# Sooner gated product in each half's last unit, moved steps in three queues, and fp16 copies of exponentials on ScalarE in the long units of the second half

## The chip, the cores and the metric

The kernel runs on one core of one Trainium2 chip. The metric is the device time of one execution in microseconds (us): 1716.42 us for the kernel before, the median of three runs (1714.65 to 1716.99).

Engines are named as in the profile: PE is TensorE (matmuls), PEld its weight loads, DVE is VectorE, ACT is ScalarE, POOL is GpSimd, SP is SyncE, which starts the transfers. L12 is line 12 of the kernel before, unless a sentence says that a line number is of the changed kernel.

## The reference

An input x of 2048 rows and 576 columns goes through two branches, and a gate per row mixes them:

```python
g = _sigmoid((x * gate_w).sum(-1, keepdims=True))
a = _A_ref(x, A_wq, A_wk, A_wv, A_wo, A_beta)
b = _B_ref(x, B_w_gate, B_w_up, B_w_down)
return g * a + (1 - g) * b
```

Branch A is attention with 32 heads of width 18, in four segments of 512 rows. In a segment each head does causal softmax attention, and mixes it with a read of a memory that holds phi(k)^T v of the segments before; a matmul with wo ends the branch. Branch B is `(silu(x @ w_gate) * (x @ w_up)) @ w_down` with an inner width of 4608.

## The kernel before, in words

One program does four stages on one core, and PE is meant to run through all of them.

**Segments (0 to 233.5 us).** For each of the four segments come nine chains `qk` (14 matmuls of 512 columns into one of three shared banks of PSUM, L223), whose results ACT and DVE turn into queries, keys and phi of both (L455 to L468), and then eight `v_step` with `mem_step`. Beside the chains of segments 1 to 3, `upd_gen` adds the last segment to the memory: PE transposes phi (L513, L516), the pieces are copied to `kt` by ACT (512 columns, L514) and DVE (the last 64 columns, L517), and PE multiplies `kt` with the values (L505). Also beside the chains, pieces of x are summed on POOL and split into fp16 pairs on ACT and DVE for the next stage: `first_sum`, `first_split`, `rest_sum` (POOL, L654), `rest_split` (ACT L248, DVE L249). Tables such as `RSTEP`, `FSUM` and `FSPLIT` say beside which chain each stands.

**First half (233.5 to 921.5 us).** The inner width is cut in 36 units f of 128, and the rows in two halves of 1024. A unit makes the gate and up products of a half by seven products of a Strassen-like scheme: `seven(t, j)` is product j, seven matmuls of 512 columns (L1426, L1429). Copies of finished products go to ACT (L1519, L1526, L1533, L1537, with SiLU L1540 and L1542), sums to DVE (L1530, L1538). After product 6, DVE forms the two parts of the gated product, `sg0` from bank and silu (L1548) and `sg1` from `p5` and silu (L1549; product 6 is not read there). `split_by` splits each part into fp16 high (`hh`, ACT L1295) and low (`hl`, DVE L1298) in later ticks.

Between two products stands a `tick` with eight beats k. A tick runs what `defer` put off to it, and starts steps of the plan: weights of the next unit (`w_make`: POOL L369, ACT L373, DVE L377), and the down weights: `d_look` measures them (ACT L1116), `d_scale` makes their scale (a PE step L158, then POOL), `d_split` makes three fp16 tiles `dw` (ACT L1139, DVE L1140, then L1142 on DVE or L1144 on ACT).

Every third unit (f = 3, 6, ..., 33) is long, 34 to 39 us where the others take 10.6 to 14.7. In it stand the 16 down groups of the three chunks before: a group is nine matmuls (L1162) into one of two banks, which DVE then adds into `ya` (L1171, or L1169 for the first). Unit 35 feeds a further 16, which run in it and in ten beats behind it. Attention runs inside the ticks as a generator, `att_gen`, one step at a time: scores (PE L889), maximum (DVE L907), scores again transposed (PE L1002), the exponential (ACT L1006), its fp16 copy `p1` (DVE L1102, or ACT L1104), the remainder `p2` (POOL L1106), and the products with the values (PE L1030, L1032). Score banks are three.

**Second half (921.5 to 1640 us).** The same 36 units with the other 1024 rows. Here some attention steps are "turned": the scores are kept (DVE L897), ACT takes the exponential (L943), DVE makes an fp16 copy (`c_bank`, L947), POOL the remainder (L948), a transfer transposes both, and PE multiplies (L964, L965; sums L975 on DVE). After that the output tail with wo ends the kernel at 1717 us.

`exp_table` is a small ACT activation (L1419) that brings the table of the exponential in early; SiLU needs another table, so each change of function costs an ACT_TABLE_LOAD. `gates` (L1413 and its DVE steps L1414 to L1416) forms the mixing gate, once, in unit 3 of the first half. `rest_second` prepares the last rows of x for the second half in unit 35 and the beats behind it (ACT L1388, DVE L1392, POOL sums L1381).

Of the kernel before, what the change touches and what calls it, by code (L numbers as in the profile page):

```python
# [17 lines left out]
AF = mybir.ActivationFunctionType  # L18
# [51 lines left out]
def gated_mix(ctx, tc, xT, xrest, wf, wfr, wfh, wd, wv, wo, beta, cmask, ident, bmask, out):  # L70
# [323 lines left out]
    with ExitStack() as st:  # L394
# [101 lines left out]
        def upd_gen(s):  # L496
            acc = [pair_tile([P, 3, MW]), pair_tile([P, 2, MW])]
            Mo, Mn = Mm[s % 2], Mm[(s + 1) % 2]
            for i in range(5):
# [8 lines left out]
                if i < 4:  # L508
# [8 lines left out]
                    nc.vector.tensor_copy(kt[:, 512:576], tb[:, 64:128])  # L517
# [143 lines left out]
        RSTEP = {2: (0, 3), 3: (5, -1), 4: (1, -4), 5: (4, -2), 6: (2,), 7: (-6,), 8: (6,)}  # L661
# [59 lines left out]
        def scan_load(t):  # L721
# [3 lines left out]
            if t in (21, 30):  # L725
# [3 lines left out]
        FSUM = {3: [(1, 0), (4, 0)], 4: [(2, 0), (1, 1)], 6: [(4, 1), (2, 1)], 7: [(6, 0)], 8: [(6, 1)]}  # L729
        FSPLIT = {2: [(0, 0)], 3: [(5, 0), (0, 1)], 4: [(1, 0), (4, 0)], 5: [(5, 1), (2, 0)], 6: [(1, 1), (3, 0)],  # L730
                  7: [(3, 1), (4, 1)], 8: [(2, 1)]}
        for s in range(NSEG):
            upd = upd_gen(s - 1) if s else None
            casts = []
            for n, (m, u) in enumerate(chains):
# [41 lines left out]
                qk(s, m, u, mid)  # L777
                flush(2)
# [19 lines left out]
            for n in range(8):  # L798
# [23 lines left out]
                else:  # L822
                    if n == 4:
                        wraw_of[1] = [w_load(1, u) for u in range(2)]
                    if n < 2:
                        first_split(6, n)
# [8 lines left out]
                    for _ in range((0, 0, 2, 1, 2, 2, 2, 2)[n]):  # L835
                        if start[0][0] < 8:
                            start.pop(0)[1]()
# [5 lines left out]
    with ExitStack() as st:  # L843
# [101 lines left out]
        def c_bank(u, n):  # L945
            lg, pq = homes["lg"][n], spot("pq", u, n)
            nc.vector.tensor_copy(pq[:, 0:L], lg)  # L947
# [103 lines left out]
        def att_gen():  # L1051
            N = 10 * NB
            for tau in range(N + TL + VL + 5):
# [44 lines left out]
                if 0 <= z < N and z // 5 not in turned:  # L1098
                    pe = cur.pop(z)
                    p1 = ap.tile([P, L], F16, name="p1", bufs=6)  # L1100
                    if later[0] or z % 5 not in turn_of[0]:
# [188 lines left out]
        later = [False]  # L1290
        turn_of = [()]
# [33 lines left out]
        def feed(half, f):  # L1325
            return [(f // CH, i, hf, hs, ds, half) for i in range(8) for hf in range(2)]
# [43 lines left out]
        def rest_second(rest):  # L1370
# [19 lines left out]
            def low(j):  # L1390
# [3 lines left out]
            todo = [(-1, load, 0), (0, high, 0), (0, high, 3), (1, low, 0), (1, low, 3), (4, load, 1), (11, high, 5),  # L1394
                    (11, total, 1), (12, low, 5), (12, high, 1), (13, total, 4), (13, low, 1), (14, total, 2),
                    (14, high, 4), (15, low, 4), (15, total, 6), (16, high, 2), (16, low, 2), (17, high, 6), (18, low, 6)]
# [37 lines left out]
        for pos, (half, f) in enumerate(seq):  # L1434
# [49 lines left out]
            def tick():  # L1484
# [5 lines left out]
                if half == 0:  # L1490
# [3 lines left out]
                    if (f == 2 and k < CH) or (f > 2 and q == 0 and 2 <= k < 2 + CH):  # L1494
                        d_look(k if f == 2 else f + k - 2)
                    if (f, k) == (2, 3) or (f > 2 and (q, k) == (0, 5)):
                        d_scale(f // CH)
                    if (f, k) == (2, 7) or (f > 2 and (q, k) == (1, 3)):
                        d_back(f // CH)
                    if f == 2 and k > 4 or f > 2 and (q, k) in ((1, 1), (1, 7), (2, 5 + int(f < FT - 1))):  # L1500
                        g = k - 5 if f == 2 else f - 1 if k == 1 else f
# [8 lines left out]
            later[0] = half == 1 and f > 0  # L1510
            turn_of[0] = () if pos < 24 else (1, 3)
# [154 lines left out]
```

## Time and profile before

| what | value |
|---|---|
| median of three runs | 1716.42 us (1714.65 to 1716.99) |
| the profiled execution | 1718.78 us |
| its span, first to last instruction | 1717.1 us |
| PE busy | 1679.5 us, 98% of the span |
| DVE busy | 1353.8 us, 79% |
| ACT busy | 1076.6 us, 63% |
| POOL busy | 889.2 us, 52% |
| mean granted PE clock | 0.998 |

The span leaves 1.68 us of the profiled execution outside. Busy shares are means over stages with different limits, so the prediction reads them stage by stage. A timeline row gives the start in us from the span's start, the duration in us, engine, line, operation and tiles, and in brackets how long the engine was idle before and what ended the wait. A row of a wait table gives who waited for whom, the sum in us, how often, and the longest.

### The profile page before, as it was taken

Reading aid. Unit: us, or ns where it says so; the run is one execution under the profiler, and the core shown is the slowest. Engines: PE = TensorE matmul, PEld = TensorE weight load, DVE = VectorE, ACT = ScalarE, POOL = GpSimd, SP = SyncE. Lnnn points to the kernel's source line nnn. Section 1 sums busy time; section 2 is a strip of 40 time slices with the busy share of each in tenths; the row PEclk is TensorE's granted clock in tenths of the full one; section 3 lists DMA queues with packets and bytes.
Section 4 is the critical chain, followed back from the end, with each engine's and each line's share of the span. In section 5 each row is a group of like instructions: output and inputs, shape, how many; then the busy total and the mean of one; then the engine's idle time right before and its main releaser. Section 6 shows DMA issues by size and latency. Waiting matters only on the chain.

```text
span 1717.1 us, 35318 instructions
## 1 busy us (share of the span) xinstructions
PE 1679.5 (98%) x12269; PEld 1077.8 (63%) x12269; DVE 1353.8 (79%) x3295; ACT 1076.6 (63%) x1930; POOL 889.2 (52%) x1191
## 2 busy tenths in 40 slices
PE   9999999999999999999999999999999999999999
PEld 7898865556655665565555656556656656655577
DVE  6687676789888988898886878788878788776466
ACT  7666567777777777767774654665556566565411
POOL 3336562266667665665452665465546565554121
PEclk9999999999999999999999999999999999999999
DMA  8666675666776675446535486796696597574544
GB/s 282 218 232 222 214 260 208 208 200 177 231 223 208 168 244 192 154 121 195 169 123 164 114 192 158 163 219 136 147 215 166 121 221 167 140 163 125 156 157 145
DMA packets 349542, 314.25 MB, mean 183 GB/s; under 512 B 201268, under 2 KB 266548, under 8 KB 349364
## 3 DMA queue, kind: packets, MB, share of 16 engines
q1 hardware_dynamic: 349364, 312.00, 63.5%
q8 instruction: 96, 1.57, 0.4%
q14 instruction: 82, 0.67, 0.1%
HBM read 186.15 MB, written 99.55 MB: 166 GB/s over the span
## 4 chain that ended last, share of the span: by engine, by line
PE 73%; DVE 12%; ACT 7%; issue 3%; DMA 3%; POOL 1%; SPq 1%; DVEq 0%; ACTq 0%; POOLq 0%
PE bank L1426 31%; PE bank L1162 18%; PE bank L223 8%; PE bank L1429 5%; PE bank L889 3%; PE bank L1002 2%; DVE ya L1171 1%; PE bank L1030 1%; ACT L1540 1%; DVE junk L907 1%; PE bank L1032 1%; PE bank L964 1%; DVE p L1102 1%; ACT row L1540 1%; DMA rc<-rt 1%
## 5 line engine op out<-in xcount | busy, mean ns | idle before, releaser
L1162 PE MATMUL bank<-dw,hh 128*128 128x320 f16 (+1 forms) x2304 | 437.5, 286 | 13.3 <-DVE ya L1171 8.9
L1162 PE MATMUL bank<-dw,hl 128*128 128x320 f16 (+1 forms) x1152 | 330.1, 287 | 3.8 <-DVE hl L1298 3.2
L1106 POOL TENSOR_TENSOR p<-pe,p 128x512 f16<-128x512 f32 x220 | 271.9, 1236 | 75.3 <-DVE p L1102 50.6
L1162 PEld LDWEIGHTS <-hh 128*128 128x128 f16 x2304 | 225.3, 98 | 99.9 <-issue 18.1
L1006 ACT ACTIVATE pe<-bank 128x512 f32<-128x512 f32 x220 | 130.1, 592 | 183.6 <-PE bank L1002 167.5
L1171 DVE SCALAR_TENSOR_TENSOR ya<-bank,sc,ya 128x320 f32<-128x320 f32 x352 | 176.2, 511 | 55.0 <-PE bank L1162 53.3
L1429 PE MATMUL bank<-xr,rh 128*128 128x512 f16 x504 | 191.0, 379 | 0.0
L907 DVE CUSTOM_DVE_ANT_0 junk<-bank,cm 128x128 bf16<-128x128 f32 (+2 forms) x352 | 169.3, 481 | 13.7 <-PE bank L889 7.3
L1298 DVE SCALAR_TENSOR_TENSOR hl<-hh,row 128x512 f16<-128x512 f16 x144 | 129.7, 902 | 45.7 <-ACT hh L1295 44.8
L1014 POOL TENSOR_SCALAR_AFFINE_SELECT pe<-pe 128x256 f32<-128x256 f32 (+1 forms) x220 | 89.3, 406 | 144.9 <-ACT pe L1006 137.3
L1162 PEld LDWEIGHTS <-hl 128*128 128x128 f16 x1152 | 112.7, 98 | 34.3 <-DVE hl L1298 3.8
L889 PE MATMUL bank<-kst,qst 108*128 108x512 bf16 (+3 forms) x512 | 124.5, 299 | 3.6 <-ACT pe L1006 2.9
L1002 PE MATMUL bank<-qst,kst 111*128 111x512 bf16 (+3 forms) x352 | 103.2, 300 | 1.1 <-DVE acc L975 1.1
L1102 DVE CAST p<-pe 128x512 f16<-128x512 f32 x203 | 103.3, 510 | 0.0
L369 POOL TENSOR_TENSOR ws<-raw 128x256 f32<-128x256 f32 x72 | 65.6, 912 | 63.4 <-DMA raw<-in_wf_dram 32.2
L1538 DVE TENSOR_TENSOR row<-bank,row 128x512 f32<-128x512 f32 x72 | 49.6, 689 | 60.9 <-ACT bank L1537 60.8
L223 PE MATMUL bank<-xo,qhi 128*128 128x512 f32 x288 | 92.5, 401 | 1.3 <-ACT xo L132 0.7
L466 POOL TENSOR_TENSOR q<-qr,q 128x512 bf16<-128x512 f32 x36 | 47.8, 1329 | 84.8 <-ACT q L465 77.0
L1295 ACT ACTIVATE hh<-row 128x512 f16<-128x512 f32 x144 | 89.0, 618 | 3.7 <-DVE row L1548 3.0
L1533 ACT ACTIVATE row<-bank 128x512 f32<-128x512 f32 x72 | 42.9, 596 | 73.7 <-PE bank L1429 73.7
L1537 ACT ACTIVATE bank<-bank 128x512 f32<-128x512 f32 x72 | 41.9, 581 | 72.8 <-PE bank L1429 70.9
L1429 PEld LDWEIGHTS <-rh 128*128 128x128 f16 x504 | 49.3, 98 | 59.6 <-issue 0.2
(1102 smaller groups left out, 4213.9 us busy)
## 6 DMA issues: line engine op xcount, KB each, us to landing
xo<-in_wf_dram SPq DMA_DIRECT2D x65, 320.0 KB
raw<-in_wf_dram SPq DMA_DIRECT2D x72, 256.0 KB
dc<-dw SPq DMA_DIRECT2D x36, 432.0 KB
dw<-dc SPq DMA_DIRECT2D x36, 432.0 KB
rh<-rc SPq DMA_DIRECT2D x72, 168.0 KB
draw<-in_wd_dram SPq DMA_DIRECT2D x36, 288.0 KB
xo<-in_xT_dram SPq DMA_DIRECT2D x33, 256.0 KB
vd<-vps SPq DMA_DIRECT2D x8, 912.0 KB
```

The costliest lines, as they stand in the source:

```text
L223: nc.tensor.matmul(t, st[n], mv[n], start=(n == 0), stop=(n == 13))
L889: nc.tensor.matmul(t[:, c:c + w], qs[:KR, pr, P * i:P * i + P], ks[:KR, pr, 0:w], start=True, stop=True)
L907: nc.vector.tensor_tensor_reduce(junk.bitcast(BF)[:, :w], t[:, c:c + w], cm[:, L - w:L], 1.0, -3.0e38, OP.add, OP.max, m[:, k:k + 1])
L1002: nc.tensor.matmul(t[:, c:c + w], ks[:KR + 3, pr, P * j:P * j + P], qs[:KR + 3, pr, P * j:L], start=True, stop=True)
L1006: nc.scalar.activation(pe, t, AF.Exp, scale=SCALE)
L1102: nc.vector.tensor_copy(p1, pe)
L1106: nc.gpsimd.tensor_sub(p2, pe, p1)
L1162: nc.tensor.matmul(t, p, d[:, q, cs], start=(f == CH * c and n == 0), stop=(f == CH * c + CH - 1 and n == 2))
L1171: nc.vector.scalar_tensor_tensor(ya[:, i, cs], t, inv[c], ya[:, i, cs], op0=OP.mult, op1=OP.add)
L1298: nc.vector.scalar_tensor_tensor(lo, hi, -STEP, src, op0=OP.mult, op1=OP.add)
L1426: nc.tensor.matmul(t, w[:, p, z], x[z][:, q], start=first and n == 0, stop=False, skip_group_check=True)
L1429: nc.tensor.matmul(t, rem[:, RPOS[j]], XR[j], start=False, stop=True, skip_group_check=True)
```

## The change

It has six parts, of which none changes what is computed:

- A: the copy of the last 64 columns of `kt` goes from DVE to ACT (12 copies).
- B: in segment 2, `rest_sum(6)` starts one chain sooner, and `rest_split(6)` stands behind chain 8 rather than in its middle.
- C: in segment 3, `first_split(2, 1)` and `first_sum(6, 1)` move from chain 8 to the first two `v_step`, `first_split(6, .)` two steps later, and the weights of unit 0 are made a step sooner.
- D: in the long units of the second half (`calm`), the copies of `c_bank` and `p1` go from DVE to ACT: 60 of 100 of the former, 68 of the latter.
- E: in unit 35 of each half, the second part of the gated product (`p5` times silu) is formed ahead of product 6, split first, and the down groups of that part come first; in the first half the last `d_split` starts three beats sooner, and the later items of `rest_second` two beats later.
- F: in the first units, `d_look` goes from unit 2 to unit 1, `d_scale` two beats sooner; the early load of the exponential's table is left out in units 0 and 3, and in unit 3 it stands, with `gates`, behind the SiLU.

```diff
-                    nc.vector.tensor_copy(kt[:, 512:576], tb[:, 64:128])
+                    nc.scalar.activation(kt[:, 512:576], tb[:, 64:128], AF.Copy)
...
-        RSTEP = {2: (0, 3), 3: (5, -1), 4: (1, -4), 5: (4, -2), 6: (2,), 7: (-6,), 8: (6,)}
+        RSTEP = {2: (0, 3), 3: (5, -1), 4: (1, -4), 5: (4, -2), 6: (2, -6)}
...
+                if (s, n) == (2, 8):
+                    rest_split(6)
...
-                    for _ in range((0, 0, 2, 1, 2, 2, 2, 2)[n]):
+                    for _ in range((0, 1, 2, 2, 2, 2, 2, 2)[n]):
...
-            nc.vector.tensor_copy(pq[:, 0:L], lg)
+            if calm[0]:
+                nc.scalar.activation(pq[:, 0:L], lg, AF.Copy)
+            else:
+                nc.vector.tensor_copy(pq[:, 0:L], lg)
...
-                    if later[0] or z % 5 not in turn_of[0]:
+                    if not calm[0] and (later[0] or z % 5 not in turn_of[0]):
                         nc.vector.tensor_copy(p1, pe)
                     else:
                         nc.scalar.activation(p1, pe, AF.Copy)
...
-            return [(f // CH, i, hf, hs, ds, half) for i in range(8) for hf in range(2)]
+            return [(f // CH, i, hf, hs, ds, half) for i in ((4, 5, 6, 7, 0, 1, 2, 3) if f == FT - 1 else range(8))
+                    for hf in range(2)]
...
-                    if (f == 2 and k < CH) or (f > 2 and q == 0 and 2 <= k < 2 + CH):
-                        d_look(k if f == 2 else f + k - 2)
-                    if (f, k) == (2, 3) or (f > 2 and (q, k) == (0, 5)):
+                    if (f == 1 and 4 <= k < 4 + CH) or (f > 2 and q == 0 and 2 <= k < 2 + CH):
+                        d_look(k - 4 if f == 1 else f + k - 2)
+                    if (f, k) == (2, 1) or (f > 2 and (q, k) == (0, 5)):
...
-                    if f == 2 and k > 4 or f > 2 and (q, k) in ((1, 1), (1, 7), (2, 5 + int(f < FT - 1))):
+                    if f == 2 and k > 4 or f > 2 and (q, k) in ((1, 1), (1, 7), (2, 6 if f < FT - 1 else 2)):
...
+            calm[0] = half == 1 and q == 0 and f > 0
...
-            if half == 0 and q == 0 and f:
+            if half == 0 and q == 0 and f > CH:
                 exp_table()
-                if f == CH:
-                    gates()
...
-            if (half or q == 0) and not cps:
+            if (half or q == 0 and f) and not cps:
                 exp_table()
+                if half == 0 and f == CH:
+                    gates()
             tick()
             tick()
+            gated = [lambda: nc.vector.scalar_tensor_tensor(sg0, xx, hk[f // 4], sg0, op0=OP.mult, op1=OP.mult),
+                     lambda: nc.vector.scalar_tensor_tensor(sg1, p5, hk[f // 4], sg1, op0=OP.mult, op1=OP.mult)]
+            parts, first = [(hh[:, z], hl[:, z], (sg0, sg1)[z]) for z in range(2)], int(f == FT - 1)
+            if first:
+                gated[1]()
             seven(xx, 6, False)
-            nc.vector.scalar_tensor_tensor(sg0, xx, hk[f // 4], sg0, op0=OP.mult, op1=OP.mult)
-            nc.vector.scalar_tensor_tensor(sg1, p5, hk[f // 4], sg1, op0=OP.mult, op1=OP.mult)
-            split_by(2, hh[:, 0], hl[:, 0], sg0, int(q < CH - 1))
-            split_by(3, hh[:, 1], hl[:, 1], sg1)
+            gated[0]()
+            if not first:
+                gated[1]()
+            split_by(2, *parts[first], int(q < CH - 1))
+            split_by(3, *parts[1 - first])
```

Three places show how the order moves. The first is ACT where unit 3 of the first half begins; these are the rows before, from the down weights of chunk 0 to the first high part of the gated product:

```order
L1139 ACTIVATE dw<-draw,sc 128x576 x2
L373 ACTIVATE wo__3111<-ws,sc 128x512
L1144 ACTIVATE dw<-dw 128x576
L1139 ACTIVATE dw<-draw,sc 128x576
L1519 ACTIVATE bank_3120<-bank_3118 128x512
L1419 ACT_TABLE_LOAD
L1419 ACTIVATE bg<-idt 128x1
L1413 ACTIVATE gg<-gl 128x16
L1144 ACTIVATE dw<-dw 128x576
L1295 ACTIVATE hh<-row 128x512
```

And these of the changed kernel, whose line numbers stand some ten to fourteen higher:

```order
L1148 ACTIVATE dw<-draw,sc 128x576 x2
L373 ACTIVATE wo__3110<-ws,sc 128x512
L1153 ACTIVATE dw<-dw 128x576
L1148 ACTIVATE dw<-draw,sc 128x576
L1531 ACTIVATE bank_3119<-bank_3117 128x512
L1153 ACTIVATE dw<-dw 128x576
L1305 ACTIVATE hh<-row 128x512
```

The table load, the small activation behind it and the gate's exponential no longer stand between the copy of product 0 and the third down tile.

The second place is DVE in unit 35 of the first half, from the sum of L1538 to the two low parts of the gated product. Before:

```order
L1538 TENSOR_TENSOR row<-bank_11775,row 128x512
L1355 SCALAR_TENSOR_TENSOR xo_10317<-xr_10334,sc,xo_10317 128x512
L1140 SCALAR_TENSOR_TENSOR dw<-draw,sc,dw 128x576
L1548 SCALAR_TENSOR_TENSOR row<-bank_11842,sc,row 128x512
L1549 SCALAR_TENSOR_TENSOR row<-row,sc 128x512
L1142 TENSOR_SCALAR dw<-dw 128x576
L1298 SCALAR_TENSOR_TENSOR hl<-hh,row 128x512 x2
```

In the changed kernel (L1149 and L1151 are its L1140 and L1142, L1548 its L1538, L1560 its L1549, L1559 its L1548, L1308 its L1298):

```order
L1149 SCALAR_TENSOR_TENSOR dw<-draw,sc,dw 128x576
L1548 TENSOR_TENSOR row<-bank_11773,row 128x512
L1151 TENSOR_SCALAR dw<-dw 128x576
L1366 SCALAR_TENSOR_TENSOR xo_10315<-xr_10332,sc,xo_10315 128x512
L1560 SCALAR_TENSOR_TENSOR row<-row,sc 128x512
L1559 SCALAR_TENSOR_TENSOR row<-bank_11843,sc,row 128x512
L1308 SCALAR_TENSOR_TENSOR hl<-hh,row 128x512 x2
```

Both steps on the down weights now stand ahead of the gated products, and the product that doesn't read product 6 stands first.

The third place is ACT inside long unit 9 of the second half, behind its SiLU. Before:

```order
L1006 ACTIVATE pe<-bank_14925 128x512
L1006 ACTIVATE pe<-bank_14959 128x512
L1006 ACTIVATE pe<-bank_14987 128x512
L943 ACTIVATE xr_12630<-xr_12630,nb 128x512
L943 ACTIVATE xr_12631<-xr_12631,nb 128x512
L140 ACTIVATE junk,sc<-raw 128x480
L943 ACTIVATE xr_12632<-xr_12632,nb 128x128
L943 ACTIVATE xr_12632<-xr_12632,nb 128x384
```

In the changed kernel (L1015 is its L1006, L949 its L943, L1113 the copy `p1`, L954 the copy of `c_bank`):

```order
L1015 ACTIVATE pe<-bank_14923 128x512
L1113 ACTIVATE p_14941<-pe 128x512
L1015 ACTIVATE pe<-bank_14957 128x512
L1113 ACTIVATE p_14967<-pe 128x512
L1015 ACTIVATE pe<-bank_14985 128x512
L949 ACTIVATE xr_12628<-xr_12628,nb 128x512
L1113 ACTIVATE p_14996<-pe 128x512
L949 ACTIVATE xr_12629<-xr_12629,nb 128x512
L1113 ACTIVATE p_15033<-pe 128x512
L140 ACTIVATE junk,sc<-raw 128x480
L949 ACTIVATE xr_12630<-xr_12630,nb 128x128
L949 ACTIVATE xr_12630<-xr_12630,nb 128x384
```

A copy now stands between one exponential and the next. PE's order is as before, apart from the one step of `d_scale` (L158).

21 lines of the change are left out of this document (13 added, 8 removed).

## The prediction

> **What bounds the kernel now.** I first read the busy times of the stages. The columns are stretch, length, then busy us (and instructions) of PE, PEld, DVE, ACT and POOL, the granted clock and the DMA share.
>
> ```profile
> 0.00:233.50 233.50, 225.85 (x1293) 195.07 (x1294) 170.42 (x393) 148.11 (x295) 112.19 (x137) 1.00 0.69 233
> 233.50:921.50 688.00, 670.73 (x4582) 393.90 (x4581) 577.67 (x1316) 496.75 (x899) 379.66 (x530) 1.00 0.61 192
> 921.50:1640.00 718.50, 709.05 (x5791) 428.43 (x5789) 557.24 (x1501) 418.49 (x709) 382.73 (x505) 1.00 0.67 162
> ```
>
> PE is busy 97% to 99% in each, so the bound is PE's own work, and the change leaves that work alone. All that it can win is PE's idle time: 7.7, 17.3 and 9.5 us, and clock. Whom PE waited for is next in PE's wait table, cut to the rows that the change touches:
>
> ```profile
> PE bank L1162 <- DVE hl L1298: 3.2, 2, 2.1
> ...
> PE bank L505 <- DVE kt L517: 1.8, 2, 1.1
> PE bank L1426 <- ACT bank L1519: 1.7, 3, 0.6
> ...
> PE bank L550 <- DVE ph L468: 1.3, 1, 1.3
> ...
> PE bank L1162 <- ACT hh L1295: 1.1, 2, 0.9
> ...
> PE bank L158 <- ACT junk L1116: 0.3, 1, 0.3
> ```
>
> A wait costs a little more than its bracket:
>
> ```profile
> 237.26 0.59 PE L1426 MATMUL bank<-xo,wo__2633 128*128 128x512 f16 x2 [0.54 <-ACT bank L1519]
> ...
> 271.53 1.46 PE L1426 MATMUL bank<-xo,wo__3071 128*128 128x512 f16 x6 [0.64 <-ACT bank L1519]
> ```
>
> Six matmuls take 1.46 us and two 0.59, so four more take 0.87: the pace is 0.22 each, a lone one lasts 0.59 - 0.22 = 0.37, and each restart loses the difference, 0.16 us, on top. I add it to each wait. The clock is the second place to look, in two stretches around the first long unit and around unit 35:
>
> ```profile
> 273.59:277.00 3.41, 1.46 (x10) 0.65 (x8) 2.78 (x6) 2.67 (x7) 0.00 (x0) 1.00 0.89 318
> 277.00:280.42 3.41, 3.41 (x13) 1.69 (x12) 2.53 (x7) 1.23 (x3) 1.45 (x2) 0.50 1.03 392
> ...
> 901.64:905.06 3.41, 1.35 (x11) 0.90 (x10) 3.41 (x6) 2.47 (x4) 1.44 (x1) 1.00 0.27 101
> 905.06:908.47 3.41, 3.41 (x17) 2.27 (x15) 0.99 (x3) 0.00 (x0) 0.00 (x0) 0.50 0.97 291
> ```
>
> Twice PE is busy for only 1.46 and 1.35 of 3.41 us, and twice the next 3.41 us run at clock 0.50. Half of such a stretch is lost, 1.7 us.
>
> **The change, part by part.**
>
> A. Two waits for L517 hold 1.8 us, with restarts 2.1. DVE was late there because its scans stood ahead; ACT's L514, which feeds the same matmul, was not waited for in these two. On ACT the copy stands right behind L514. A copy of 64 columns isn't in the trace on ACT; between a one-column activation (0.20 us, quoted below) and one of 512 columns (0.62 us) I put it at 0.25. Value **-2.0**; from -2.1 to +3.0, if all 12 copies delayed the phi chain behind them.
>
> B. The 1.3 us of L468 come from these:
>
> ```profile
> 154.25 1.28 POOL L654 TENSOR_TENSOR xo<-xo,xo 128x512 f32<-128x512 f32 x1
> 154.31 2.77 DVE L137 SCALAR_TENSOR_TENSOR xr<-xr,sc,xr 128x384 f16<-128x384 f32 x1
> ...
> 158.30 0.74 DVE L249 SCALAR_TENSOR_TENSOR xr<-xo,sc,xr 32x512 f16<-32x512 f32 x1
> ```
>
> DVE's L137 took 2.77 us beside POOL's sum, and L249 stood between L462 and the awaited L468. Both go elsewhere. Value **-1.4**, from 0 (a chain sooner the sum stretches another DVE step) to -1.5.
>
> C. The L1519 wait of 0.54 above is in unit 0, behind a weight step L373 that now runs sooner. With its restart **-0.7**; from -0.7 to +0.7, if the moved splits delay the values' chain as long.
>
> F. Unit 3 of the first half begins so:
>
> ```profile
> 271.50 1.28 ACT L1419 ACT_TABLE_LOAD   x1
> 272.80 0.20 ACT L1419 ACTIVATE bg<-idt 128x1 f32<-128x1 f32 x1
> ```
>
> ```profile
> 275.70 0.30 PE L1162 MATMUL bank<-dw,hh 128*128 128x320 f16 x1 [1.14 <-DVE dw L1140]
> 276.59 0.30 PE L1162 MATMUL bank<-dw,hl 128*128 128x320 f16 x1 [0.59 <-DVE dw L1142]
> ```
>
> Table load and small activation delay ACT's next hh (L1295) by 1.5 us, hence L1298 and the L1140 and L1142 queued behind it on DVE. With 1.1 - 0.9 = 0.2 for L1295 (its other wait is in unit 35) the waits are 1.9, with three restarts 2.4. All three can't gain the whole 1.5, since they lie one behind the other on PE: the last, L1142, decides, and moved up by 1.5 it leaves 0.9. So -1.5. The scale starts two beats sooner, so L1139 ahead of L1519 does too: of that wait's 0.64 + 0.16 = 0.80 I take -0.35, a little under half.
>
> In unit 1 the removed load frees the third L1519 wait, 1.7 - 0.64 - 0.54 = 0.5, with restart -0.7, and the wait of L158 goes, -0.5. But two L1116 now stand ahead of unit 2's L1519:
>
> ```profile
> 260.53 0.67 ACT L1116 ACTIVATE junk<-draw 128x576 f16<-128x576 f32 x1
> ```
>
> Their 2 x 0.67 us and the reads behind them outlast the 1.28 us of the load removed there. No wait of that kind is in the trace; between 0 and 1.7 I take 0.75, near the 0.64 above. Together -1.5 - 0.35 - 0.7 - 0.5 + 0.75 = **-2.3**, from 0 to -4.
>
> Of the first stretch's 3.41 - 1.46 = 2.0 us without PE, 1.5 go with these waits. What is left is no longer than the waits at other places behind which the clock stayed 1.00, so I count the half clock gone: **-1.7**, from 0 to -1.7.
>
> E. Unit 35 of the first half:
>
> ```profile
> 901.39 0.45 PE L1162 MATMUL bank<-dw,hh 128*128 128x320 f16 x2 [0.89 <-ACT hh L1295]
> 903.90 0.31 PE L1162 MATMUL bank<-dw,hl 128*128 128x320 f16 x1 [2.06 <-DVE hl L1298]
> ```
>
> ```profile
> 899.93 0.74 DVE L1548 SCALAR_TENSOR_TENSOR row<-bank,sc,row 128x512 f32<-128x512 f32 x1
> 900.59 1.36 DVE L1549 SCALAR_TENSOR_TENSOR row<-row,sc 128x512 f32<-128x512 f32 x1
> 901.88 1.37 DVE L1142 TENSOR_SCALAR dw<-dw 128x576 f16<-128x576 f16 x1
> 903.17 1.28 DVE L1298 SCALAR_TENSOR_TENSOR hl<-hh,row 128x512 f16<-128x512 f16 x2
> ```
>
> ```profile
> 900.14 2.94 POOL L1381 TENSOR_TENSOR raw<-raw 128x512 f32<-128x512 f32 x2 [14.30 <-DVE dw L1140]
> ```
>
> PE waits 0.89 + 2.06 us, with restarts 3.3. Ahead of L1298 stood L1142, and L1549 and L1142 ran 1.36 and 1.37 us beside POOL's sums. The change takes L1142 and the sums away, and the part first needed no longer waits for product 6. Late next is that part's L1295 and L1298, some 0.2 us: **-3.1**, from -1.5 to -3.3. The half clock behind it: **-1.7**, from 0. Unit 35 of the second half has the other L1298 wait, 3.2 - 2.06 = 1.1, with restart 1.3; POOL works beside it there still, so **-0.9**, from 0 to -1.3. The down groups are the same in number, only their order differs.
>
> D. In the second half PE waits for DVE and ACT in these rows:
>
> ```profile
> PE bank L1162 <- DVE ya L1171: 4.1, 10, 0.9
> PE bank L1002 <- DVE acc L975: 1.1, 1, 1.1
> ...
> PE bank L1162 <- DVE ya L1169: 0.9, 1, 0.9
> ...
> PE bank L889 <- ACT pe L1006: 0.6, 2, 0.3
> ```
>
> This is one long unit, f = 9, as a stretch; then come ACT's exponential and DVE's copy `p1` as groups over the second half (busy, mean ns, idle before and its releasers), and ACT's copy over the whole kernel:
>
> ```profile
> 1087.42:1123.38 35.96, 34.63 (x303) 23.36 (x302) 29.04 (x83) 18.92 (x35) 18.79 (x26) 1.00 0.51 118
> ```
>
> ```profile
> L1006 ACT ACTIVATE pe<-bank 128x512 f32<-128x512 f32 x123 | 72.9, 593 | 100.0 <-PE bank L1002 86.3 <-POOL p L1106 6.1 <-POOL pe L1014 2.8
> ...
> L1102 DVE CAST p<-pe 128x512 f16<-128x512 f32 x124 | 62.4, 505 | 0.0
> ```
>
> ```profile
> L1104 ACT ACTIVATE p<-pe 128x512 f16<-128x512 f32 x17 | 10.6, 622 | 0.0
> ```
>
> Some 12 copies move per long unit: DVE loses 12 x 0.505 = 6.1 us and falls from 29.0 to 23 of 36, ACT gains 12 x 0.622 = 7.5 and rises from 18.9 to 26.4. What DVE's relief can win is 4.1 + 1.1 + 0.9 with 12 restarts of 0.16: 8.0 us. One of these waits, with DVE's queue ahead of it:
>
> ```profile
> 1116.43 0.43 PE L1162 MATMUL bank<-dw,hh 128*128 128x320 f16 x2 [0.51 <-DVE ya L1171]
> ```
>
> ```profile
> 1115.24 0.67 DVE L1102 CAST p<-pe 128x512 f16<-128x512 f32 x1
> ```
>
> The copy of 0.67 us stands right before the awaited L1171, so without it that wait goes. Other waits, the one on L975 among them, stand behind steps that stay on DVE. I take half, -4. On ACT the copies queue ahead of the next L1006, whose bank PE wants back. ACT's idle time before L1006 hides them: 86.3 us over 123, 0.70 each, more than one copy's 0.62. So **-4**, from -8.0 to +4 (one copy in 20 uncovered).
>
> **The sum.** -2.0 - 1.4 - 0.7 - 2.3 - 1.7 - 3.1 - 1.7 - 0.9 - 4 = -17.8 us. The profiled execution of 1718.78 us would become 1701.0. It stands 2.4 us above the median of 1716.42, which would become **1698.6**.
>
> The Trainium skill ("TensorE: Matmul & The Clock Gate", What's actually happening) has the half clock follow an idle window of about 3.4 us. Here 2.0 us without PE within 3.41 sufficed, so the trace differs; by the page alone neither half-clock stretch would be there to lose, and the sum would be -14.4.
>
> **Rivals.**
>
> 1. *ACT becomes the bound in the long units (slower than before).* Place: the three score banks. Behind an L1006 stand an L943 and up to two copies, 2 x 0.62, and PE's next score step waits for the bank. Price: all 128 copies uncovered would cost 128 x 0.622 = 80 us. Without D the sum is -13.8; slower by more than 0.2% (3.4 us, about what a measurement can tell from no change) begins at +17.2, 22% of the 80, or 1.7 us per long unit. At 30% the time is 1716.4 - 13.8 + 24 = 1727. For it: the two L1006 waits that are there already, and that the copies come in rows. Against: 0.70 us idle per L1006.
> 2. *D wins nothing*: the evictions L1171 are late because of their two banks, not of DVE's queue, or ACT gives back the gain. -13.8, 1702.6.
> 3. *The stalls leave, but the clock still halves*, or other waits move in at units 2, 3 and 35 (the change doesn't do what it says there): without the 3.4 us of clock and with half of E and F, -17.8 + 3.4 + 3.2 = -11.2, 1705; with D at nothing too, 1709.
> 4. *D wins all 8.0*: -21.8, 1694.6.
>
> **How the numbers follow.** The forecast (D between -6 and -2, the rest as summed) 40%, its own range 1696 to 1701; rival 2 20%, rival 3 18%, rival 4 8%, rival 1 14%, of which half ends within 0.2% and half slower. Faster by over 0.2% is thus 0.86, within 0.07, slower 0.07. The range 1692 to 1711 leaves out rival 1 and the tails.
>
> **What would show it.** Right: no PE wait on L517's successor; no wait above 0.5 us on the hl split behind unit 35; granted clock 1.00 right behind unit 3's start and unit 35; waits on L1171's successor in the second half down to some 2 us; long units of the second half 0.4 us shorter in the mean. Wrong: waits on L1006's successor in the second half well above 0.6 us, a new wait for L1519's successor in unit 2 above 1 us, or half clock in new places.

## The result, and the profile after

| | median of 5 runs | lowest to highest |
|---|---|---|
| before | 1716.99 us | 1714.65 to 1719.42 |
| changed | 1710.69 us | 1707.77 to 1712.90 |

The ratio is 0.9958, with a 95% interval of 0.9943 to 0.9972: faster by 0.42%, some 7 us, where 17.8 were forecast. The profiled execution of the changed kernel took 1707.77 us, with a span of 1705.7, and is the fastest of its five; the one of before, on which the sum was made, took 1718.78, near the slow end of its runs. So the two profiles lie 11.0 us apart, and the medians 6.3.

The stages of the changed kernel, with the columns of the first fence of the prediction (the bounds are its own first matmuls of unit 0 of each half):

```profile
0.00:229.61 229.61, 225.52 (x1294) 195.18 (x1295) 167.68 (x376) 148.79 (x305) 110.18 (x136) 1.00 0.69 235
229.61:911.82 682.21, 666.71 (x4580) 392.87 (x4580) 576.57 (x1318) 491.16 (x894) 380.55 (x531) 1.00 0.61 194
911.82:1629.00 717.18, 708.80 (x5795) 428.75 (x5793) 508.60 (x1375) 484.70 (x839) 374.10 (x505) 1.00 0.67 163
```

In the second half DVE was relieved of 49 us and ACT took on 66, as the change says. PE's idle time is 4.1 us in the first stage (7.7 before), 15.5 in the second (17.3) and 8.4 in the third (9.5). PE's wait table, cut to the rows that answer to those of before (L1437 and L1531 are the old L1426 and L1519, L1171 and L1308 the old L1162 and L1298, L1180 and L1178 the old L1171 and L1169, L895 and L1015 the old L889 and L1006, L1151 the old L1142):

```profile
PE bank L1171 <- DVE ya L1180: 6.3, 12, 1.0
PE bank L895 <- ACT pe L1015: 4.8, 11, 1.0
PE bank L1437 <- ACT bank L1531: 2.9, 3, 2.0
PE bank L1171 <- DVE ya L1178: 2.6, 2, 1.6
...
PE bank L1171 <- DVE hl L1308: 0.6, 2, 0.4
PE bank L1171 <- DVE dw L1151: 0.6, 1, 0.6
```

The waits for L517, L468, L1140 and L1295 are gone, that for the low part fell from 3.2 to 0.6 us, and that for the evictions of L1180 from 8.9 to 6.3. But the wait for the copy of product 0 rose from 1.7 to 2.9, with one of 2.0; that for evictions L1178 from 1.9 to 2.6; and that for ACT's exponentials from 2.9 to 4.8. The next table is worked out from the traces: the length in us of a unit, from its first matmul to the next unit's first, in units that differ. Some lengths repeat to 0.02 us from trace to trace, others vary by a microsecond or more. "Before" has two profiles (the second from the first experiment).

| unit | before | before, again | changed |
|---|---|---|---|
| first half, start of unit 0 at | 233.53 | 232.83 | 229.61 |
| unit 0 | 11.28 | 11.27 | 12.75 |
| units 1 + 2 + 3 | 59.30 | 58.49 | 57.52 |
| unit 35 | 34.02 | 33.74 | 29.46 |
| second half, units 0 to 33 | 688.51 | 688.49 | 687.35 |

### The profile page after: what moved, and what is told of

Same layout as the page of the kernel before. It is cut to its first block, busy times and chain, and to the rows that moved or that the text cites. A ratio compares the mean times of both kernels' runs of the same rounds, so it can differ in the third digit from the quotient of the medians.

```text
span 1705.7 us, 35389 instructions
## 1 busy us (share of the span) xinstructions
PE 1674.5 (98%) x12269; PEld 1076.9 (63%) x12269; DVE 1300.5 (76%) x3155; ACT 1137.9 (67%) x2064; POOL 879.6 (52%) x1191
## 4 chain that ended last, share of the span: by engine, by line
PE 76%; ACT 7%; DVE 7%; DMA 4%; issue 3%; POOL 1%; SPq 1%; DVEq 0%; ACTq 0%; POOLq 0%
PE bank L1437 30%; PE bank L1171 19%; PE bank L223 10%; PE bank L1440 5%; PE bank L895 3%; PE bank L1011 2%; PE bank L1039 1%; ACT L1550 1%; PE bank L505 1%; DMA raw<-in_wf_dram 1%; PE bank L1041 1%; ACT row L1550 1%; PE bank L973 1%; DVE ya L1180 1%; DVE junk L913 1%
## 5 line engine op out<-in xcount | busy, mean ns | idle before, releaser
L1171 PE MATMUL bank<-dw,hh 128*128 128x320 f16 (+1 forms) x2304 | 435.1, 285 | 9.5 <-DVE ya L1180 6.3
L1171 PE MATMUL bank<-dw,hl 128*128 128x320 f16 (+1 forms) x1152 | 329.0, 286 | 1.2 <-DVE hl L1308 0.6
L1171 PEld LDWEIGHTS <-hh 128*128 128x128 f16 x2304 | 224.8, 98 | 95.0 <-issue 15.4
L1015 ACT ACTIVATE pe<-bank 128x512 f32<-128x512 f32 x220 | 130.2, 592 | 161.8 <-PE bank L1011 149.2
L1180 DVE SCALAR_TENSOR_TENSOR ya<-bank,sc,ya 128x320 f32<-128x320 f32 x352 | 177.5, 512 | 76.3 <-PE bank L1171 74.5
L1308 DVE SCALAR_TENSOR_TENSOR hl<-hh,row 128x512 f16<-128x512 f16 x144 | 126.8, 882 | 43.6 <-ACT hh L1305 42.6
L1171 PEld LDWEIGHTS <-hl 128*128 128x128 f16 x1152 | 112.3, 97 | 30.2 <-DVE hl L1308 1.3
L895 PE MATMUL bank<-kst,qst 108*128 108x512 bf16 (+3 forms) x512 | 124.5, 299 | 5.8 <-ACT pe L1015 4.8
L1548 DVE TENSOR_TENSOR row<-bank,row 128x512 f32<-128x512 f32 x72 | 49.7, 690 | 63.8 <-ACT bank L1547 63.7
L1559 DVE SCALAR_TENSOR_TENSOR row<-bank,sc,row 128x512 f32<-128x512 f32 x72 | 53.9, 749 | 43.2 <-PE bank L1440 22.2
```

Of the source, the lines that this page charges most:

```text
L895: nc.tensor.matmul(t[:, c:c + w], qs[:KR, pr, P * i:P * i + P], ks[:KR, pr, 0:w], start=True, stop=True)
L1015: nc.scalar.activation(pe, t, AF.Exp, scale=SCALE)
L1171: nc.tensor.matmul(t, p, d[:, q, cs], start=(f == CH * c and n == 0), stop=(f == CH * c + CH - 1 and n == 2))
L1180: nc.vector.scalar_tensor_tensor(ya[:, i, cs], t, inv[c], ya[:, i, cs], op0=OP.mult, op1=OP.add)
L1308: nc.vector.scalar_tensor_tensor(lo, hi, -STEP, src, op0=OP.mult, op1=OP.add)
```

## The experiments

The experiments ran on different chips, so medians are compared by their ratios to the runs of before made on the same chip beside them; 0.001 is 1.7 us. A bracket behind a ratio is its 95% interval, some 2 us to each side, so differences of 2 us between two variants are not shown by the times alone. Variants without a part are edits of the changed kernel. In those without C the lines behind it stand four lower: L1433, L1527, L1167, L1174 and L891 are the changed kernel's L1437, L1531, L1171, L1178 and L895.

**The kernel before, again.**

> The kernel before, unchanged, for a second profile and more times. Theory (half the missing gain is in the runs, not in the change): stretches of half clock come and go with the phase of the clock's window, so the runs' granted clocks spread from 0.998 to 1.000 and the times over some 4 us, and the second profile shows the same waits of PE within 0.1 us each but not both half-clock stretches. Rival (the two stretches belong to the kernel): the second profile has both again, at units 3 and 35 of the first half, and every run has clock 0.998.

The two lots of runs agree: ratio 0.9999 (0.9989 to 1.0008). The second profile has the waits that the change goes after (L1298, L517, L1519, L468, L1140, L1295, L1142, L158) within 0.1 us of the first's; others differ by up to 1.1 us, and one eviction wait of 0.95 us at 285 us is new. It has one half-clock stretch, behind unit 35; none at unit 3. Of the 17 runs of before beside it, one had a mean clock of 1.000, ten 0.999, five 0.998 and one 0.997, and a half-clock stretch lowers the mean by 0.001; their times spread from 1713.07 to 1720.82, with a median of 1718.16. So the theory holds for unit 3 and the rival for unit 35, and the profile on which the sum was made, with two stretches and 0.998, had more of them than most runs.

**Without C.**

```diff
-                    if n == 0:
-                        first_split(2, 1)
-                    if n == 1:
-                        first_sum(6, 1)
-                    if 2 <= n < 4:
-                        first_split(6, n - 2)
+                    if n < 2:
+                        first_split(6, n)
...
-                    for _ in range((0, 1, 2, 2, 2, 2, 2, 2)[n]):
+                    for _ in range((0, 0, 2, 1, 2, 2, 2, 2)[n]):
```

(and chain 8 gets its split and its sum back.)

> The changed kernel without part C. Theory (C loads the last value steps): the wait in unit 0 for the copy of product 0, 2.0 us in the changed kernel, falls to 0.4 to 0.7 us, unit 0 is 1.5 us shorter than 12.75 us, and the time about 1.5 us below the changed kernel's. Rival (the value steps' chain on DVE and ACT ends when it ends, and PE's gain from A and B is handed back there): the wait stays at 1.8 us or more and the time within 0.5 us.

Median 1706.4 us, ratio 0.9934 (0.9921 to 0.9946) against the changed kernel's 0.9958 (0.9943 to 0.9972): without C the kernel is 4.1 us faster by these ratios, though the two intervals just touch. The wait in unit 0, in the changed kernel and without C:

```profile
234.81 1.46 PE L1437 MATMUL bank<-xo,wo__2592 128*128 128x512 f16 x6 [2.02 <-ACT bank L1531]
```

```profile
234.09 1.46 PE L1433 MATMUL bank<-xo,wo__2633 128*128 128x512 f16 x6 [0.68 <-ACT bank L1527]
```

Unit 0 is 11.54 us instead of 12.75. The theory holds for the wait, and about for the unit (1.2 us, where 1.5 were expected). The 4.1 us are more than that; part of them is clock, since the mean clock is 0.9990 over the five runs of the changed kernel and 0.9998 over the six without C, and 0.0008 is 1.4 us.

**Which half of C: the splits back in place, or the weights.** The run `no_c_split` has the splits and the sum put back as above, chain 8 included, and the weights still a step sooner; `no_c_start` has the last piece of the diff alone.

> The changed kernel with the splits and the sum of part C put back (in chain 8 and the first two value steps); the weights of unit 0 still start a step sooner. Theory (each weight step put between a value step's link and the next lengthens their chain through ACT and DVE): the wait in unit 0 stays at 1.5 us or more and unit 0 at 12.4 us or more, since a weight step L373 still stands between the last two value steps on ACT. Rival (the moved splits load the value steps): the wait falls to 0.8 us as without C, unit 0 to 11.5 us.

> The changed kernel with only the weights of unit 0 back at their old step; the splits and the sum stay moved. Theory (the weight steps lengthen the chain): the wait in unit 0 falls to 0.9 us or less, unit 0 to 11.6 us or less, the time to within 1.5 us of the 1706.4 us without C. Rival (the moved splits do it): the wait stays above 1.5 us, the time near 1710.

With the splits back, ratio 0.9938 (0.9923 to 0.9953); with only the weight steps back, 0.9945 (0.9932 to 0.9958). The times lie too close to tell, the waits don't. With the splits back and the weights still sooner:

```profile
234.02 1.45 PE L1433 MATMUL bank<-xo,wo__2592 128*128 128x512 f16 x6 [0.91 <-ACT bank L1527]
```

With the weights back and the splits still moved, PE waits three times in the same unit:

```profile
231.87 1.04 PE L1437 MATMUL bank<-xo,wo__2590 128*128 128x512 f16 x4 [0.40 <-DVE wo__2590 L377]
...
234.06 1.04 PE L1437 MATMUL bank<-xo,wo__2633 128*128 128x512 f16 x4 [0.51 <-DVE wo__2633 L377]
...
236.00 1.24 PE L1437 MATMUL bank<-xo,wo__2633 128*128 128x512 f16 x5 [0.68 <-ACT bank L1531]
```

Unit 0 is 11.64 us in the one, 12.68 in the other. For unit 0 the rival holds: the moved splits make it long. My theory falls there, but not for the chain itself. From the first L491 of the eight value steps to the last, ACT's timeline has 15.47 us without C, 16.18 with the sooner weights alone, 16.62 with the moved splits alone and 17.29 with both: the weight steps lengthen the chain too, by 0.7 us, of which PE feels 0.1 in unit 0, and the splits by 1.15.

**Only piece 6 later.** The same as without C, but with

```diff
-                    if n < 2:
-                        first_split(6, n)
+                    if 2 <= n < 4:
+                        first_split(6, n - 2)
```

> The changed kernel with C left out except that the two splits of piece 6 stand in value steps 2 and 3 rather than 0 and 1; the split and the sum of chain 8 are where they were before. Theory (any split put later among the value steps is still being worked off when PE leaves them): the wait in unit 0 is 1.6 us or more, unit 0 at 12.4 us or more. Rival (what was brought over from chain 8 is the surplus): the wait stays at 0.8 us, unit 0 at 11.6.

The wait is 0.68 us, unit 0 11.49, the ratio 0.9942 (0.9928 to 0.9956). The rival holds again: the later place does no harm in unit 0; the surplus is the split and the sum brought over from chain 8. ACT's timeline among the value steps shows what such a step does. In a value step ACT copies (L484, L485), waits for DVE (L486), and makes the next piece (L491). In the changed kernel:

```profile
220.68 0.46 ACT L491 ACTIVATE vps<-r 128x288 bf16<-128x288 f32 x1 [0.58 <-DVE r L486]
221.03 0.70 ACT L136 ACTIVATE xo<-ph,sc 128x512 f16<-128x512 f32 x1
221.64 0.71 ACT L373 ACTIVATE wo__2555<-raw,sc 128x512 f16<-128x512 f32 x1
...
223.54 0.46 ACT L491 ACTIVATE vps<-r 128x288 bf16<-128x288 f32 x1 [0.58 <-DVE r L486]
```

And without C, a little later in the stage:

```profile
223.46 0.46 ACT L491 ACTIVATE vps<-r 128x288 bf16<-128x288 f32 x1 [0.58 <-DVE r L486]
223.81 0.70 ACT L373 ACTIVATE wo__2590<-raw,sc 128x512 f16<-128x512 f32 x1
...
225.71 0.46 ACT L491 ACTIVATE vps<-r 128x288 bf16<-128x288 f32 x1 [0.58 <-DVE r L486]
```

A value step is a closed loop through ACT and DVE: from L491 to L491 it takes 1.64 us with nothing put in (221.82 to 223.46 without C), 2.25 with a weight step L373 in it and 2.86 with a split L136 as well. So a step of 0.70 us makes the loop 0.6 us longer, though ACT is idle for 0.58 us in each round. PE has no new wait there, since it runs ahead: it begins unit 0 4.2 us before the last L491 starts (229.61 and 233.81; without C 2.4 us, 230.10 and 232.50). The arrears come due in unit 0, where the copy of product 0 starts right behind that last L491, at 234.17.

**Without D.** `calm` is never set.

```diff
-            calm[0] = half == 1 and q == 0 and f > 0
+            calm[0] = False
```

> The changed kernel without part D (all copies of the second half's long units on DVE again). Theory (D hands its gain back as waits for ACT and POOL): in the second half the waits for evictions and reductions rise to about 6 us, those for ACT's exponentials and POOL's remainders fall to about 1.3, the eleven long units together change by 0.5 to 2 us, and the time by less than 2 us. Rival (D is worth 4): the long units are 4 us longer in sum.

Median 1710.79, ratio 0.9958 (0.9945 to 0.9971), the changed kernel's own. Units 0 to 33 of the second half take 688.43 us instead of 687.35, so D wins 1.1 us, and the eleven long units together 1.5 us, on the theory's side. The other traces agree: the same units take 688.40 to 688.55 in the four other traces without D, and 687.33 to 688.21 in the seven others with the whole of it. PE's waits from unit 0 to unit 35 of the second half, without D and then with it:

```profile
PE bank L1171 <- DVE ya L1180: 4.1, 10, 0.9
PE bank L1011 <- DVE acc L984: 1.1, 1, 1.1
PE bank L1171 <- DVE ya L1178: 0.8, 1, 0.8
...
PE bank L895 <- ACT pe L1015: 0.6, 2, 0.3
```

```profile
PE bank L1171 <- DVE ya L1180: 2.4, 5, 1.0
PE bank L895 <- ACT pe L1015: 2.4, 5, 1.0
PE bank L1011 <- DVE acc L984: 1.1, 1, 1.1
```

Evictions (L1180 and L1178) fall from 4.9 to 2.4 us, exponentials rise from 0.6 to 2.4, and the remaining rows have the same sums. Two of the five waits for exponentials, 0.7 us, are those that stood there without D; three are new. The longest of them is in long unit 3 of that half. L1550 and L1552 are the two SiLU, L954 and L1113 the copies of `c_bank` and `p1`. ACT does this there without D:

```profile
971.45 0.60 ACT L1015 ACTIVATE pe<-bank 128x512 f32<-128x512 f32 x1 [1.26 <-POOL xo L957]
972.06 1.28 ACT L1550 ACT_TABLE_LOAD   x1
...
976.06 0.58 ACT L1015 ACTIVATE pe<-bank 128x512 f32<-128x512 f32 x1
```

and this with D, where PE's wait follows:

```profile
971.36 0.60 ACT L1015 ACTIVATE pe<-bank 128x512 f32<-128x512 f32 x1 [0.22 <-PE bank L1011]
971.85 0.62 ACT L954 ACTIVATE xo<-xo 128x512 f16<-128x512 f32 x1
972.37 0.62 ACT L1113 ACTIVATE p<-pe 128x512 f16<-128x512 f32 x1
973.01 1.28 ACT L1550 ACT_TABLE_LOAD   x1
...
977.02 0.58 ACT L1015 ACTIVATE pe<-bank 128x512 f32<-128x512 f32 x1
```

```profile
977.65 0.38 PE L895 MATMUL bank<-kst,qst 108*128 108x128 bf16 x2 [1.03 <-ACT pe L1015]
```

From the first table load to the next exponential ACT has no idle time: load, two SiLU, load, small activation, 4.0 us in either kernel. Two copies that queue ahead of this chain move the exponential behind it by 1.05 us, and PE waits 1.03. The other two new waits, 0.29 us in unit 6 and 0.45 in unit 12, stand behind the same chain with one copy ahead of it (L954 in the one, L1113 in the other). Elsewhere the copies cost PE less than 0.1 us at an exponential.

**One kind of copy each** (both without C).

```diff
-                    if not calm[0] and (later[0] or z % 5 not in turn_of[0]):
+                    if later[0] or z % 5 not in turn_of[0]:
```

is `nc_d_c`, with only the `c_bank` copies on ACT; `nc_d_p` has `if False:` in place of `if calm[0]:` in `c_bank`, so that only `p1` is on ACT.

> Without C, and of D only the copies p1 on ACT; the copies of c_bank stay on DVE. Theory (D's gain and its loss come from different copies; p1 stands between two exponentials L1006 whose bank PE awaits, so p1 brings the ACT waits): the second half's long units keep waits on ACT's exponentials of 2 us or more, and the stage of the second half is within 1 us of the kernel before's. Rival (the c_bank copies bring them): those waits fall to the 0.9 us of the kernel without D, and the stage is 2 us shorter than before's.

> Without C, and of D only the copies of c_bank on ACT; p1 stays on DVE. Theory (p1 brings the ACT waits): waits on ACT's exponentials in the second half at 1 us or less, waits for evictions below the 6 us of the kernel without D, and the stage 1.5 to 2.5 us shorter than before's. Rival: the c_bank copies bring the ACT waits, and the stage is no shorter than before's.

Units 0 to 33 of the second half take 687.33 us with `p1` alone and 686.64 with `c_bank` alone: each kind alone wins as much as both or more (1.1 and 1.8 us), and the last run below has 686.53 with `c_bank` alone again. PE waits 1.6 us for exponentials in both. Neither theory nor rival holds as put: both kinds bring ACT waits, though the stage with `c_bank` alone is 1.9 us shorter than before's, as the theory had it. What they lose adds up and what they win doesn't: in unit 3, with one copy ahead of the table load, PE waits 0.52 us in the one and 0.50 in the other, where both copies cost 1.03; the wait in unit 6 is there with `c_bank` alone, the one in unit 12 with `p1` alone. Evictions, 4.9 us without D, fall to 3.0 and to 2.7 with one kind and only to 2.4 with both. Ratios: 0.9941 (0.9926 to 0.9956) and 0.9936 (0.9921 to 0.9951).

**Without F, and without C and F.** The lines of F are put back as before.

> The changed kernel without part F. Theory (F's gain is handed back in unit 3, where the copy of product 4 queues on ACT behind squares that wait for their transfer): units 1 to 3 of the first half together are at most 1 us longer than the 57.5 us of the changed kernel, half-clock stretches left out, and the eviction wait of 1.6 us in unit 3 falls below 1 us, since PE comes there later. Rival (F is worth its forecast): units 1 to 3 are 2.3 us longer or more, and the eviction wait stays.

> The changed kernel without C and without F. Theory (F itself is worth its forecast of 2 to 4 us, and C's wait hid it, since with C the runs with and without F differ by 0.5 us): the time is 2 to 4 us above the 1706.4 us without C alone, and runs with half clock return. Rival (F is worth nothing, its waits are replaced by those behind ACT's squares): the time is within 1 us of 1706.4.

Beside C, F is worth nothing: ratio 0.9957 (0.9945 to 0.9969). Units 1 to 3 take 58.70 us without F, with one half-clock stretch of 1.7 in them, against 57.52, and the eviction wait of 1.6 us is gone, so the first theory holds. Without C it is 0.9949 (0.9936 to 0.9963) without F and 0.9934 with it, 2.6 us, with intervals that overlap, and three of five runs are below a clock of 1.000 against one of six; the theory that C hid F is favoured and not settled. The same four ratios give C 1.4 us where F is left out. The waits show where F's gain went. From 240 to 300 us PE waits in the kernel before:

```profile
PE bank L1426 <- ACT bank L1519: 1.2, 2, 0.6
PE bank L1162 <- DVE dw L1140: 1.1, 1, 1.1
PE bank L1162 <- DVE ya L1169: 1.0, 1, 1.0
PE bank L1162 <- DVE dw L1142: 0.6, 1, 0.6
PE bank L158 <- ACT junk L1116: 0.3, 1, 0.3
PE bank L1162 <- ACT hh L1295: 0.2, 1, 0.2
```

and in the changed kernel:

```profile
PE bank L1171 <- DVE ya L1178: 2.6, 2, 1.6
PE bank L1437 <- ACT bank L1531: 0.9, 2, 0.7
PE bank L1171 <- DVE dw L1151: 0.6, 1, 0.6
PE bank L1437 <- ACT row L1552: 0.4, 1, 0.4
```

4.4 us before (4.1 in the changed kernel without F), 4.5 after. The new one of 1.6 us is at 283 us, and ACT's timeline points at its cause:

```profile
280.40 0.74 ACT L140 ACTIVATE xo<-xo 128x640 f32<-128x640 f32 x1 [0.75 <-DMA xo<-in_wf_dram]
...
281.13 0.58 ACT L1547 ACTIVATE bank<-bank 128x512 f32<-128x512 f32 x1
```

ACT sits in front of a square of weights (L140) until its transfer lands; behind it stands the copy of product 4, behind that DVE's sum, and behind that the awaited eviction.

**The weights to be squared, sooner.** Without C, and in unit 3's case the first four blocks are loaded two ticks sooner.

```diff
-            return [((-2, -1, 0, 1, 3, 4, 4, 5)[k], load),
+            return [((-2, -1, 0, 1, 3, 4, 4, 5)[k] - (sooner if k < 4 else 0), load),
```

> The changed kernel without C, and with the first four weight blocks that ACT squares in unit 3 loaded two ticks sooner. Theory (F's gain is handed back since ACT's squares wait for their transfer, with the copies of products 3 and 4 behind them): ACT no longer waits over 0.5 us for those transfers, the eviction waits of unit 3, 1.3 + 1.6 + 1.0 us without C, fall below 1.5 us in sum, and unit 3 to 33.5 us or less. Rival (the transfers are bound by bandwidth, or the evictions by DVE): they land as late as before relative to the squares, and unit 3 stays above 34 us.

From 265 to 300 us PE waits, without C and then with the sooner loads:

```profile
PE bank L1167 <- DVE ya L1174: 3.5, 3, 1.4
PE bank L1167 <- DVE dw L1147: 0.6, 1, 0.6
```

```profile
PE bank L891 <- DMA kst<-stk: 1.6, 2, 0.8
PE bank L1167 <- DVE dw L1147: 0.6, 1, 0.6
```

All the eviction waits are gone, so when those blocks land did decide them, though ACT still waits 1.5 and 1.0 us for two of those transfers, ahead of the place that matters. Unit 3 takes 33.72 us instead of 35.52, between the two forecasts. A load of attention keys is late in their place by 1.6 us. The ratio, 0.9929 (0.9917 to 0.9942), can't be told from that without C.

**E alone, and A with B alone**, on the kernel before.

> The kernel before with part E alone. Theory (E is worth what was forecast, a wait of 3.1 us, the half clock behind it and 0.9 us in the second half): unit 35 of the first half is 4.3 us shorter than 33.7, none of its waits exceeds 0.5 us, no half clock behind it, the last unit's wait in the second half falls from 1.1 to 0.4 us, and the time falls by 4.5 to 6 us. Rival (the next unit hands it back): units 0 and 1 of the second half are longer, and the time falls by 2 us or less.

> The kernel before with parts A and B alone. Theory (three waits of PE go, and unit 0 takes most of it through): no wait for the 64-column copy nor for the phi sum of chain 8, unit 0 begins 3.2 us sooner than in the kernel before from the same start, its own wait rises from 0.5 to at most 0.9 us, and the time falls by 2 to 3.5 us. Rival (the value steps are bound by ACT and DVE, and hand it back): the wait in unit 0 rises to 2 us, and the time falls by 1.5 us or less.

E: median 1712.76, ratio 0.9968 (0.9956 to 0.9980), 5.5 us. Unit 35 takes 30.32 us, 3.4 to 3.7 less than in the two profiles of before, where 4.3 were expected; no half clock stands behind it, and five of its six runs have a clock of 1.000. One wait for the low part of 1.1 us is left there, where at most 0.5 was expected, none in the last unit of the second half, and the kernel from that unit to the end is 1.2 us shorter. The theory holds in the time, against the rival. A and B: ratio 0.9988 (0.9977 to 0.9999), 2.1 us. The waits for L517 and L468 are gone and unit 0 begins at 230.07, with a wait of 0.68 us, as forecast; but of the 3.5 us by which unit 0 begins sooner than in the first profile of before, units 0 to 3 take back 1.0 and units 4 to 34 another 0.9. In unit 3, 36.92 us long, PE finds the waits of before, the one for L1142 0.5 us longer; it is as long with E alone, so coming sooner isn't what makes it so. Of eleven runs one has a clock of 1.000, three 0.999, three 0.998 and four 0.997, a mean of 0.9981 against 0.9985 for the runs of before beside it, which is 0.7 us.

**The best of these.** Without C, with the sooner loads and only the `c_bank` copies on ACT.

> As the run before, and with only the c_bank copies of D on ACT, p1 back on DVE. If both findings hold, unit 3 is 33.5 us or less, the second half 1.8 us shorter than before's, and the time near 1704, below the changed kernel and all variants so far. If the sooner loads do nothing, the time is that of the run with c_bank copies alone, near 1707.

Median 1705.83 (1704.53 to 1706.04), ratio 0.9924 (0.9912 to 0.9937), all five runs at clock 1.000: faster than before and than the changed kernel, and not to be told from the other kernels without C. Unit 3 takes 33.47 us, units 0 to 33 of the second half 2.0 us less than before; both expectations hold, and the ratio makes 1704 us of the 1716.99.

## Why the prediction was right and wrong, step by step

- **A and B, -3.4.** Right on their waits, which are gone; worth 2.1 us alone (0.2 to 3.9 by the interval), since later units take some back and the clock was a little lower.
- **C, -0.7. This step failed, with its sign.** I saw one weight step ahead of L1519 and took its wait as gone, with +0.7 at worst for the moved splits. The price of a step put into the value steps' loop was not asked: each adds 0.6 us to it, the splits as moved 1.15 in all, and PE pays in unit 0, 12.75 us long against 11.54 without C. Over the three kernels with F that keep the moved splits (0.9958, 0.9945, 0.9958) and the five without them and without the sooner loads (0.9934, 0.9938, 0.9941, 0.9936, 0.9942) the mean times differ by 2.7 us, and by 2.3 if the kernel without D, one of the three, is left out. I take 2.7 for C; 4.1, from one pair of kernels, has 1.4 us of clock in it. Of the 2.7, 1.2 stand in unit 0 and some 0.7 in unit 2 (12.1 to 12.5 us with the moved splits, 10.9 to 12.1 without). The rest is not placed, and why unit 2 is longer isn't shown. Over these kernels the clock doesn't give it: 11 of 16 runs were at 1.000 with the moved splits, 17 of 25 without.
- **F, -2.3 and -1.7. This step failed too.** The waits named went, as put (0.6 us was left for L1142, where 0.9 was taken). What is late next was asked only for the copy of product 0 in unit 2 (0.71 us, where 0.75 was taken), not for unit 3, where squares on ACT wait for their transfers and an eviction behind them costs 1.6 us: a term put at nothing. Beside C nothing was left, without it 2.6 us, uncertain.
- **E, -3.1, -1.7 and -0.9.** Right: 5.5 us alone (3.4 to 7.6) against 5.7. Unit 35 itself gave 3.4 to 3.7 alone and 4.3 to 4.6 in the changed kernel, where the wait for the low part left there is 0.2 us. The wait in the second half fell from 1.1 to 0.4 us.
- **D, -4.** Right in sign, wrong in size: -1.1 us, and the long units are 0.14 us shorter in the mean, where 0.4 was forecast. The relief was sized well: waits for evictions fell by 2.5 us and by six in number, 3.5 us with the restarts of 0.16, where 4 was taken. The term that failed is the cover on ACT, which put the price at nothing: 0.70 us ahead of each L1006 was a mean over 123, and ahead of the exponentials behind the two SiLU there is none: instead a chain of 4.0 us without a gap stands there. Waits for exponentials rose by 1.8 us and by three in number, 2.3 with restarts, and the three new ones stand there. 3.5 less 2.3 is about the 1.1 measured. Rival 1's mechanism is there, at some 2% of its price of 80 us.
- **The clock, -3.4 in all.** Both stretches stood in one profile. Unit 35's was in each profile without E and in none with it. Unit 3's came and went without F, and with F it came once more, behind an eviction wait of 2.26 us (the run with only piece 6 later). With C one can come at unit 0, as in the profile without F. Of the five runs of the changed kernel only the profiled one was at 1.000.

Measured apart, the parts come to -2.1 + 2.7 - 5.5 - 1.1 and 0 to -2.6 for F, -6.0 to -8.6 in sum, against -7.2 together. So of the 10.6 us that the forecast had too much, C has 3.4, D 2.9, A and B 1.3, and F with its clock 1.4 to 4.0. Rival 3 with D at nothing had -7.2 as well, by luck: it gave up half of E, which came in full, and knew nothing of C.

## What to carry to other kernels

An engine's share of idle time in a stage doesn't say that a step can be put there: look whether the stage is a closed loop between two other engines (L491, L484, L485, L486 here), since here such a loop grew by 0.6 us for every step of 0.7 us put into it, and the bill came at the next place that waits. When a wait of the bound engine goes, write down what the next stage's transfers do when it arrives sooner. And average idle time covers nothing by itself: a queue's cover has to be read at each place where the moved steps stand, and above all where a chain without a gap, here two table loads with SiLU between them, stands ahead of what the bound engine awaits.

## What the runs showed of the hardware

The half clock came behind a stretch of 3.41 us with PE idle for more than half of it, not only behind an idle one. Three pairs of stretches, from the profiles without F (two) and with E alone:

```profile
232.81:236.22 3.41, 1.40 (x8) 0.58 (x6) 2.59 (x10) 2.83 (x8) 1.65 (x3) 1.00 0.78 263
236.22:239.64 3.42, 3.42 (x10) 1.22 (x8) 1.36 (x3) 0.32 (x1) 2.75 (x4) 0.50 0.68 257
273.77:277.19 3.42, 1.68 (x12) 1.15 (x13) 3.42 (x7) 2.22 (x6) 1.10 (x2) 1.00 0.93 303
277.19:280.60 3.41, 3.41 (x11) 1.32 (x10) 1.55 (x6) 1.56 (x5) 0.73 (x1) 0.50 1.01 394
```

```profile
272.57:275.98 3.41, 1.84 (x10) 0.80 (x9) 1.97 (x3) 3.41 (x9) 0.04 (x1) 1.00 1.01 342
275.98:279.40 3.42, 2.51 (x17) 1.66 (x17) 3.42 (x10) 1.47 (x4) 1.45 (x2) 1.00 1.04 393
```

The sixteen traces, cut into such stretches by the clock's own records, have nine stretches at 0.50 before PE's last matmul. In the stretch ahead of each, PE was busy for 0.60 to 1.68 us (18 to 49%); behind the least busy ones of the others, from 1.82 us (53%) on, the clock stayed 1.00. What lies between isn't shown. Behind PE's last matmul two traces differ: 1.44 and 1.63 us were followed by 1.00, where PE had nothing left to run. Where the bounds of these stretches fall differs from run to run, so a wait of 2 us falls into one stretch in some runs and into two in others. The waits at unit 3 leave PE busy for 1.46 us of a stretch in the first profile of before and for 1.98 in the second, and only the first has half clock behind it. The same kernel then runs at a mean clock of 1.000 to 0.997, and every 0.001 is 1.7 us.
